# Fused attention and expert routing: score buffers in a fixed turn, and the fill between score groups by a written list

## The chip, the cores and the metric

The kernel runs on one core of a Trainium2 chip, in one launch. The metric is device time in microseconds. The kernel before was timed three times: 424.58, 422.84 and 422.7 us, median 422.84. The profile was taken in a further execution, whose own time was 424.22 us.

A core has five engines that run side by side, each through its own instructions in a fixed order: TensorE (PE: matmuls; PEld: its weight loads), VectorE (DVE), ScalarE (ACT), GpSimd (POOL) and SyncE (SP). They wait for one another by semaphores. Matmul results go to PSUM, which has eight banks.

## The reference

```python
# q, k, v: (8 batches, 8 heads, 1152, 64); w1: (8, 512, 1024); w2: (8, 1024, 512)
q_pool = q.reshape(B, H, S // 2, 2, D).mean(axis=3)          # 576 queries
scores = scale * q_pool @ k.transpose(0, 1, 3, 2)            # 576 x 1152
attn   = softmax(scores)                                     # (with exp(scores - max))
x      = (attn @ v), tokens x 512                            # 4608 tokens
for e in range(8):                                           # each token has one expert
    h = relu(x[domain_id == e] @ w1[e])
    out[domain_id == e] = h @ w2[e]
```

## The kernel before

**Attention.** Two heads form a pair; there are 32 pairs (4 to a batch), and each takes 12 steps of 432 score columns, 384 steps in all. One step is `score(t)` (PE: the keys' and queries' product for both heads, in the upper and lower half of the array, into a two-bank PSUM tile `s`) and `expo(t)` (ACT: one exponential over 2 x 432 columns from `s` into the SBUF tile `e`). The pool `spsum` holds three such two-bank tiles, so six of the eight banks. Once per pair `turn` transposes the next pair's keys and queries (30 transposes, L566) into one more `s` tile, and DVE copies them out (L571, L576).

**Products.** `av(p, h, c)` multiplies chunk c of the exponentials by the values (five matmuls, L619) into the single-bank tile `acc`; after nine chunks `evac` (DVE, L632 and L634) divides by the row sum, and `acc` is free for the next head.

**Expert work in the attention.** Tokens are sorted to 128-row tiles by expert, five per expert. Tiles whose tokens are in finished batches are gathered (POOL, `get_x`) and computed during the attention, in the remaining PSUM bank (tile `px`). One such tile is 17 pieces of PE work: one transposition (L783), eight `up` pieces (four matmuls each, L801) and eight `down` pieces (one matmul each, L814). After the transposition, after each four `up` pieces and after the last `down` piece DVE empties `px` (L786, L806, L820) before the next piece can start.

**What sets the order.** The program writes the PE's order as a loop over steps. Steps come in windows of two: both `score`s of a window stand together (L595; with the `turn` between them in the window that has it), then come three products and as many pieces as a planner allows. The planner (class `Fill` and the loop around `room`) keeps a sum of estimated costs per window and carries a debt. Products lag nine steps behind their scores (`AVS`), three in each window. `GET` holds the steps at which tiles are gathered. Scores use one tile form of PE (64 rows), products and pieces another (128 rows).

**After the attention** the remaining tiles run by expert in runs of one to five tiles: `stage1` (L1058, 32 matmuls a run for up to 512 columns), `stage2` (L1103, eight matmuls a tile), with tiles of coming runs transposed in between (L1076). 13 tiles are done in the attention, 27 after it, in runs of 3, 1, 2, 2, 2, 2, 3, 2, 5, 5.

Of the kernel before, what the change touches and what calls it, by code (L numbers as in the profile page):

```python
# [19 lines left out]
def kernel(  # L20
# [14 lines left out]
    E, _, F = moe_w1.shape  # L35
    NC = S // P
    NF = F // P
    ND = Dm // P
# [36 lines left out]
    spsum = att.enter_context(tc.tile_pool(name="spsum", bufs=3, space=bass.MemoryType.PSUM))  # L75
# [84 lines left out]
    pre = spsum.tile([P, 2, 512], FP32, name="s")  # L160
# [398 lines left out]
    def turn(p):  # L559
        kp, qp = kpt[p], qpt[p]  # L560
        new_kq(p)
        mt = spsum.tile([P, 2, 512], FP32, name="s")[:, :, :].bitcast(F16)
# [23 lines left out]
    def score(t):  # L586
        p, s_ = divmod(t, SPP)
        s = spsum.tile([P, 2, 512], FP32, name="s")
        st[t] = s
        o, u = 0, W * s_  # L590
        while o < W:
            c, q0 = divmod(u + o, Sp)
            n = min(Sp - q0, W - o)
            for r, (lo, hi) in enumerate(HALF):
                nc.tensor.matmul(  # L595
                    s[:, r, o : o + n], lhsT=kq[p][lo:hi, c * P : (c + 1) * P],
                    rhs=qz[p % 2][lo:hi, q0 : q0 + n], start=True, stop=True,
                )
            o += n
# [11 lines left out]
    def av(p, h, c, pool):  # L611
        if c == 0:
            if pool[0] is spsum:
                acc[p, h] = spsum.tile([P, 2, 512], FP32, name="s")[:, 0, :]
# [67 lines left out]
    def load_part(e, j):  # L682
# [6 lines left out]
    AVS = {9 + 2 * g: [(g // 3, c, ACC) for c in range(3 * (g % 3), 3 * (g % 3) + 3)] for g in range(6)}  # L689
    LAST = (spsum, "s")  # L690
    AVS_END = {
        8: [(0, c, ACC) for c in range(4)],
        10: [(0, c, ACC) for c in range(4, 6)],
        12: [(0, 6, ACC)] + [(1, c, LAST) for c in range(7)] + [(0, 7, ACC), (1, 7, LAST), (0, 8, ACC), (1, 8, LAST)],
    }
    STEP, C_MODE, C_S, C_T, C_AV, C_X, C_P, LAG = 771, 190, 183, 440, 147, 220, 217, 250
    SPAN = {2: 1420, 4: 1700, 6: 1260}
# [50 lines left out]
    class Fill:  # L748
        def __init__(self):
            self.blocks, self.cur, self.ready = [], None, 0  # L750

        def open(self):
            return self.cur is not None or (self.blocks and self.blocks[0][3])

        def piece(self):
            if self.cur is None:
                self.cur = list(self.blocks.pop(0))
            self.cur[0].pop(0)()
            if not self.cur[0]:
                self.ready = now[0] + self.cur[2]  # L760
                self.cur = None

        def able(self, t):
            b = self.blocks[0] if self.blocks else None
            return b and (b[3] or b[4].get("t", NST) < t < NST - 8 and t >= WSTEP[b[4]["xs"][0]][3] + 14)

        def turns(self, t):
            h0 = tiles[len(turned0)] if len(turned0) < len(tiles) else None
            if h0 and len(turned0) <= len(begun) and got.get(h0["xs"], NST) + 10 <= t < NST - 13:
                return h0  # L770
            return None

    fb = Fill()

    turned, turned0, begun, tiles = [], [], [], []
# [13 lines left out]
    def add_tile(e, i):  # L789
        h0 = {"xs": (e, i)}  # L790
        tiles.append(h0)
# [33 lines left out]

        for fn, lo, hi in ((up, 0, 4), (up, 4, NF), (down, 0, NF)):
            fb.blocks.append((
                [lambda f=f, fn=fn: fn(f) for f in range(lo, hi)], 222, 1, (fn, lo) != (up, 0), h0
            ))
# [5 lines left out]
    GET = [112, 118, 140, 168, 188, 208, 213, 230, 248, 266]  # L835
    want = [(e, i, at) for (e, i), at in zip(early, GET)]
    want += [(FILL, 0, 296), (0, 2, 304), (FILL, 1, 310), (FILL, 2, 316), (1, 2, 322), (2, 2, 328)]
    want += [(e, 2, 334) for e in range(3, E) if e != FILL]
# [46 lines left out]
    windows = {}  # L885
    for t in range(0, NST, 2):
        p, s_ = divmod(t, SPP)
        turns = [-(p + 1)] if s_ == (8 if p < 2 else 4) and p + 1 < NPAIR else []
        windows[t] = [t, *turns, t + 1]

    debt = 0
    for t in range(NST + 4):
# [14 lines left out]
        work_ns, span = 0, 0  # L907
        for it in windows.get(t, ()):
            if it < 0:
                turn(-it)  # L910
                work_ns += C_T
            else:
                score(it)
                expo(it)
                work_ns += C_S
                span += STEP
        if span:
            work_ns += C_MODE
            for off in (0, SPP):
                p0 = p - off // SPP  # L920
                if 0 <= p0 < NPAIR:
                    avs = AVS_END if p0 == NPAIR - 1 else AVS
                    work_ns += C_AV * sum(len(avs.get(s_ + off + d_, ())) for d_ in (0, 1))
            span = SPAN.get(s_, span) if 1 < p < NPAIR - 1 else span
        if t == 1:
            rest_k()
        for off in (0, SPP):
            p0 = p - off // SPP
            if 0 <= p0 < NPAIR:
                avs = AVS_END if p0 == NPAIR - 1 else AVS  # L930
                for h, c, bank in avs.get(s_ + off, ()):
                    av(p0, h, c, bank)
                    if c == NC - 1:
                        evac(p0, h)
                        if p0 % HP == HP - 1 and h == 1:
                            for i in range(NQ):
                                if p0 < NPAIR - 1:
                                    put[t + 1 + i] = (p0 // HP, i)
                                else:
                                    put_x(p0 // HP, i)  # L940

        if t == NST - 2 and not fb.open() and len(turned0) < len(tiles):
            x_ = tiles[len(turned0)]
            if got.get(x_["xs"], NST) + 10 <= t:
                x_["xt"] = fill.tile([P, ND, P], F16, name="xt0")
                turn_x(x_["xt"][:, :, :], *x_["xs"])
                turned0.append(x_["xs"])
                x_["t"] = t
        if t == NST + 1:
            while fb.open():  # L950
                fb.piece()
# [15 lines left out]
        while main and span:  # L967
            room = (180 if p > 1 and s_ in SPAN else LAG) + span - debt - work_ns
            if fb.cur is None:
                if t < fb.ready:  # L970
                    break
                x_, able = fb.turns(t), fb.able(t)
                if x_ and room >= C_X and not (able and room >= 2 * C_P):
                    x_["xt"] = fill.tile([P, ND, P], F16, name="xt0")
                    turn_x(x_["xt"][:, :, :], *x_["xs"])
                    turned0.append(x_["xs"])
                    x_["t"], fb.ready = t, t + 1
                    work_ns += C_X
                    break
                if not able:  # L980
                    break
            if room < C_P:
                break
            fb.piece()
            work_ns += C_P
# [377 lines left out]
```

## Time and profile before

| what | value |
|---|---|
| median of three runs | 422.84 us (422.7 to 424.58) |
| the profiled execution, own time | 424.22 us |
| its span, first to last instruction | 422.1 us |
| PE / ACT / DVE busy | 390.8 / 338.2 / 230.7 us |
| mean granted TensorE clock | 0.986 |
| last exponential ends | 315.99 us |
| first matmul of the last phase | 316.75 us |

The span divides in two at about 316 us: the attention, in which ACT is busy almost without a break, and the expert phase, in which PE is. Matmul times in the profile overlap and their ends are modelled; how long PE needs for a group is read from the start of one group to the start of the next. For ACT the time from the end of one exponential to the end of the next says more than the length of one, since consecutive ones overlap.

### The profile page before, as it was taken

How to read it: one execution, taken by the hardware profiler on the slowest of the kernel's cores; microseconds unless marked ns; L12 is line 12 of the kernel's file. 1: busy time of each engine (PE TensorE's matmuls, PEld its weight loads, DVE VectorE, ACT ScalarE, POOL GpSimd, SP SyncE). 2: the span in 40 equal slices, each digit the busy share in tenths (PEclk: the TensorE clock that was granted, in tenths of full speed). 3: DMA queues.
4: the chain of work that ended last, by engine and by line, in shares of the span. 5: the costliest groups of instructions: out<-in, count | busy, mean ns of one | idle time of the engine just before them, and what ended most of it. 6: DMA issues, size and time to landing. Idle time of an engine off the chain costs nothing.

```text
span 422.1 us, 14534 instructions
## 1 busy us (share of the span) xinstructions
PE 390.8 (93%) x6282; PEld 260.3 (62%) x6282; DVE 230.7 (55%) x635; ACT 338.2 (80%) x451; POOL 185.4 (44%) x303
## 2 busy tenths in 40 slices
PE   7888888888999999999999999999999999999992
PEld 4555555555766766766767667666675767555451
DVE  4588779884555565556565656556424345333231
ACT  5999999999999999999999999999992434323220
POOL 5542222423462734155423335644605888542422
PEclk9699999999999999999999999999999999999997
DMA  8999999994999999959689485986862697999302
GB/s 213 213 233 226 225 239 234 215 226 93 210 211 261 246 220 238 255 121 248 135 217 178 100 186 122 231 177 163 149 117 83 139 221 204 185 157 159 124 27 97
DMA packets 53134, 77.02 MB, mean 182 GB/s; under 512 B 12623, under 2 KB 41840, under 8 KB 53058
## 3 DMA queue, kind: packets, MB, share of 16 engines
q0 software_dynamic: 38336, 66.80, 78.1%
q1 hardware_dynamic: 14450, 9.06, 9.6%
q8 instruction: 51, 0.84, 0.8%
q14 instruction: 25, 0.20, 0.2%
q10 hardware_dynamic: 272, 0.13, 0.1%
HBM read 95.46 MB, written 15.21 MB: 262 GB/s over the span
## 4 chain that ended last, share of the span: by engine, by line
PE 44%; ACT 42%; issue 5%; DVE 4%; DMA 2%; POOL 1%; SPq 0%; POOLq 0%; ACTq 0%; DVEq 0%
ACT e L607 41%; PE hp L1058 11%; PE op L1103 11%; PE acc L619 7%; PE s L595 7%; PE px L801 3%; PE px L814 2%; DMA q<-in_q_dram 1%; DVE xb L634 1%; PE s L566 1%; PE hp L1076 1%; DMA x_tok<-xb 1%; DVE osb L452 0%; DVE h L440 0%; SPq L649 0%
## 5 line engine op out<-in xcount | busy, mean ns | idle before, releaser
L607 ACT ACTIVATE e<-s 128x864 f16<-128x864 f32 x384 | 305.1, 939 | 3.9 <-PE s L595 3.5
L595 PE MATMUL s<-qz,kq 64*128 64x432 f16 (+2 forms) x1152 | 119.9, 288 | 13.8 <-ACT e L607 10.3
L619 PE MATMUL acc<-v,e 128*128 128x65 f16 x2835 | 119.5, 194 | 4.9 <-DVE xb L634 4.1
L619 PEld LDWEIGHTS <-e 128*128 128x128 f16 x2880 | 104.2, 98 | 32.3 <-DVE xb L634 14.1
L595 PEld LDWEIGHTS <-kq 64*128 64x128 f16 x1152 | 48.6, 94 | 42.6 <-issue 24.7
L516 POOL DMA_INDIRECT out_dram<-osb,gid x40 | 42.2, 1056 | 72.8 <-DVE osb L820 38.9
L660 POOL DMA_INDIRECT xs<-x_tok,grow x40 | 42.8, 1069 | 69.8 <-DVE xs L94 26.8
L115 POOL DMA_DIRECT2D vs<-in_v_dram x32 | 23.8, 742 | 61.4 <-DVE v L541 28.9
L1103 PE MATMUL op<-w2h,hT 128*128 128x512 f16 x208 | 47.5, 379 | 0.0
L1058 PE MATMUL hp<-xt,w1h 128*128 128x256 f16 (+3 forms) x352 | 43.6, 282 | 0.2 <-ACT hT L1063 0.2
L1058 PEld LDWEIGHTS <-w1h 128*128 128x128 f16 x384 | 33.7, 98 | 15.8 <-DVE xs L94 0.4
L571 DVE COPY kq<-s 128x1152 f16<-128x1152 f16 x31 | 23.5, 757 | 34.5 <-PE s L566 34.5
L1065 DVE TENSOR_SCALAR hT<-hp 128x256 f16<-128x256 f32 (+3 forms) x40 | 20.7, 517 | 36.9 <-PE hp L1058 30.0
L1109 ACT COPY osb<-op 128x512 f32<-128x512 f32 x15 | 8.8, 586 | 39.6 <-PE op L1103 39.6
L1063 ACT ACTIVATE hT<-hp 128x256 f16<-128x256 f32 (+3 forms) x40 | 18.3, 459 | 24.3 <-PE hp L1058 24.2
L801 PE MATMUL px<-xt,w1h 128*128 128x128 f16 x416 | 34.0, 221 | 0.6 <-issue 0.6
L632 DVE RECIPROCAL cum<-acc 128x5 f32<-128x5 f32 x47 | 9.0, 191 | 43.9 <-PE acc L619 43.8
L1103 PEld LDWEIGHTS <-hT 128*128 128x128 f16 x208 | 19.8, 98 | 20.9
L814 PE MATMUL px<-w2h,h 128*128 128x512 f16 x104 | 32.3, 385 | 0.0
L801 PEld LDWEIGHTS <-w1h 128*128 128x128 f16 x416 | 23.4, 98 | 12.8 <-issue 12.8
L532 DVE TENSOR_TENSOR qp<-q 96x768 f16<-96x768 f32 x31 | 29.3, 946 | 2.4 <-DMA q<-in_q_dram 2.4
L806 DVE TENSOR_SCALAR h<-px 128x512 f16<-128x512 f32 x26 | 18.0, 691 | 15.2 <-PE px L801 14.2
(148 smaller groups left out, 337.3 us busy)
## 6 DMA issues: line engine op xcount, KB each, us to landing
q<-in_q_dram POOLq DMA_DIRECT2D x28, 576.0 KB
vs<-in_v_dram POOLq DMA_DIRECT2D x32, 288.0 KB
k<-in_k_dram POOLq DMA_DIRECT2D x31, 288.0 KB
w1h<-in_moe_w_dram POOLq DMA_DIRECT2D x16, 512.0 KB
w2h<-in_moe_w_dram POOLq DMA_DIRECT2D x16, 512.0 KB
x_tok<-xb SPq DMA_DIRECT2D x23, 96.0 KB, 6.0
q<-in_q_dram SPq DMA_DIRECT2D x3, 576.0 KB, 6.8
x_tok<-xb SPq DMA_DIRECT2D x23, 64.0 KB, 5.8
```

Of the source, the lines that this page charges most:

```text
L115: nc.gpsimd.dma_start(vs[:, :, :, :], v[b, h : h + 2].rearrange("h (p c) d -> p h c d", p=P))
L516: ins = nc.gpsimd.indirect_dma_start(out=dst[:, :], out_offset=bass.IndirectOffsetOnAxis(ap=ap, axis=0), in_=src, in_offset=None, **kw,)
L532: nc.vector.tensor_tensor(out=qp[0:QP, :, :, :].rearrange("p j h d -> p h j d"), in0=q2[:, :, :, 0:D], in1=q2[:, :, :, D : 2 * D], op=ALU.add,
L571: nc.vector.tensor_copy(kq[p][:, :].rearrange("p (c r k) -> p r c k", c=NC, r=2), mt[:, :, 0 : NC * 64].rearrange("p r (c k) -> p r c k", ...
L595: nc.tensor.matmul(s[:, r, o : o + n], lhsT=kq[p][lo:hi, c * P : (c + 1) * P], rhs=qz[p % 2][lo:hi, q0 : q0 + n], start=True, stop=True,)
L607: nc.scalar.activation(e_[:, :, o : o + W], st.pop(t)[:, :, 0:W], AF.Exp, bias=0.0, scale=0.0625)
L619: nc.tensor.matmul(acc[p, h][:, i * (D + 1) : (i + 1) * (D + 1)], lhsT=et[p, c // 3][:, h, o : o + P], rhs=v16[p % NV][:, c, h, 0 : D + 1] ...
L660: nc.gpsimd.indirect_dma_start(out=dst, out_offset=None, in_=x_dram[0 : 1 + nb * Sp, :], in_offset=bass.IndirectOffsetOnAxis(ap=ap, axis=0),)
L801: nc.tensor.matmul(m[:, f % 4, :], lhsT=wts[e][0][:, cc, f * P : (f + 1) * P], rhs=h0["xt"][:, cc, :], start=cc == 0, stop=cc == ND - 1,)
L814: nc.tensor.matmul(h0["o"][:, :], lhsT=h0["h"][:, f, :], rhs=wts[e][1][:, f, :], start=f == 0, stop=f == NF - 1,)
L1058: nc.tensor.matmul(hp_[:, lo : lo + n], lhsT=w1h[:, cc, f * P : (f + 1) * P], rhs=xt[:, cc, lo : lo + n], start=cc == 0, stop=cc == ND - 1,)
L1103: nc.tensor.matmul(op_[:, :], lhsT=hT[:, f, i * P : (i + 1) * P], rhs=w2h[:, f, :], start=f == 0, stop=f == NF - 1,)
```

## The change

The edit has three parts.

- **Buffers.** `spsum` has one buffer per name now, and three tiles s0, s1, s2 are made once; `next_s()` hands them out strictly in turn to scores, transposes and the last accumulators.
- **Order.** The planner, `AVS`, `AVS_END` and the cost constants are gone. From step 108 on a list of strings gives, for each window of two steps, what stands on PE: A is one product, P one piece (the transposition counts as one), a number repeats the letter before it, and what stands ahead of a slash goes between the window's two scores. Rows of six strings are one pair. Before step 108 each window has three products, as before. Two of its 23 lines are shown in the diff.
- **Tiles.** 14 tiles are computed in the attention, 26 after it, and some tiles are gathered at other steps (`GET`, `want`).

```diff
-    spsum = att.enter_context(tc.tile_pool(name="spsum", bufs=3, space=bass.MemoryType.PSUM))
+    spsum = att.enter_context(tc.tile_pool(name="spsum", bufs=1, space=bass.MemoryType.PSUM))
...
-    pre = spsum.tile([P, 2, 512], FP32, name="s")
+    sbuf = [spsum.tile([P, 2, 512], FP32, name=f"s{i}") for i in range(3)]
+    used = [1]
+    pre = sbuf[0]
+
+    def next_s():
+        used[0] += 1
+        return sbuf[(used[0] - 1) % 3]
...
-        mt = spsum.tile([P, 2, 512], FP32, name="s")[:, :, :].bitcast(F16)
+        mt = next_s()[:, :, :].bitcast(F16)
...
-        s = spsum.tile([P, 2, 512], FP32, name="s")
+        s = next_s()
...
+    PLAN0 = 108
+    PLAN = (
...
+        "A6 P3A3 A3 A2/PA P4A A4P "
+        "A4P2 P2A5 P2 A2/A2 P2A4 P5 "
...
+    ).split()
...
-    GET = [112, 118, 140, 168, 188, 208, 213, 230, 248, 266]
+    GET = [112, 124, 143, 162, 180, 208, 220, 238, 256, 274]
...
+        if main and t % 2 == 0:
+            line = PLAN[(t - PLAN0) // 2] if t >= PLAN0 else "A3" if t >= 8 else "-"
+            inner, _, line = line.rpartition("/")
+            score(t)
+            expo(t)
+            if s_ == (8 if p < 2 else 4) and p + 1 < NPAIR:
+                turn(p + 1)
+            steps(t, inner)
+            score(t + 1)
+            expo(t + 1)
+            steps(t, line)
...
+        if t == NST:
+            left = [u[1:] for u in units]
+            lead = [u for u in left if u < (0, 7)] + [u for u in left if (1, 0) <= u < (1, 7)]
+            for h, c in lead + [(0, 7), (1, 7), (0, 8), (1, 8)]:
+                product(t, (NPAIR - 1, h, c), LAST if h else ACC)
```

How the instructions stand at three places follows.

On PE, pair 23, steps 6 and 7 of the pair, so the first window behind the one with the transposes; `s` is the score tile, `kq` and `qz` the keys and queries, `px` a piece, `acc` a product, and the brackets name the engine whose semaphore is waited for. Before:

```order
L595 MATMUL s<-qz_100,kq 128x144
L595 LDWEIGHTS kq
L595 MATMUL s<-qz_100,kq 128x432 [waits Activation_49]
L595 LDWEIGHTS kq
L595 MATMUL s<-qz_100,kq 128x432
L814 LDWEIGHTS h_5479
L814 MATMUL px<-w2h,h_5479 128x512
L619 LDWEIGHTS e
L619 MATMUL acc<-v_0_103,e 128x65
```

Now (s_122 is the tile of step 6, s_123 the one into which the transposes went; ten product matmuls stand in the gap):

```order
L602 MATMUL s_122<-qz_100,kq 128x144
L626 LDWEIGHTS e
L626 MATMUL acc<-v_0_103,e 128x65
...
L602 LDWEIGHTS kq
L602 MATMUL s_123<-qz_100,kq 128x432 [waits DVE_49]
L602 LDWEIGHTS kq
L602 MATMUL s_123<-qz_100,kq 128x432
L626 LDWEIGHTS e
```

Step 7's score waited for an exponential (that of step 5) and directly followed step 6's; it now stands two products later, and waits for DVE's copies of the transposes instead.

On DVE, the same pair, around those copies (`kq`, `qz`); `cum` and `xb` are the division after nine products, `h` and `osb` empty `px`, `qp`, `v` and `kp` prepare coming pairs. Before:

```order
L541 COPY v_1_104<-vs 128x2x9x64
L547 COPY kp<-k_5232 128x2x9x64
L632 RECIPROCAL cum<-acc 128x5
L634 TENSOR_TENSOR xb<-acc,cum 128x5x64
L571 COPY kq<-s 128x2x9x64
L576 COPY qz_99<-s 128x6x64
L576 COPY qz_99<-s 128x6x32
L632 RECIPROCAL cum<-acc 128x5
```

Now:

```order
L548 COPY v_1_104<-vs 128x2x9x64
L554 COPY kp<-k_4967 128x2x9x64
L639 RECIPROCAL cum<-acc 128x5
L641 TENSOR_TENSOR xb<-acc,cum 128x5x64
L807 TENSOR_SCALAR h_5431<-px 128x512
L578 COPY kq<-s_123 128x2x9x64
L583 COPY qz_99<-s_123 128x6x64
L583 COPY qz_99<-s_123 128x6x32
L639 RECIPROCAL cum<-acc 128x5
```

In this pair one emptying of `px` has moved ahead of the copies; it belongs to pieces that stand five products and two scores ahead of the transposes on PE.

On ACT, in the last phase, the runs over experts 3 to 5 (`hT` after stage1 with the run's columns, `xt` a transposed tile, `osb` an output tile). Before:

```order
L1063 ACTIVATE hT<-hp 128x256 x4
L1082 COPY xt<-hp 128x4x128
L1109 COPY osb_8593<-op 128x512
L1063 ACTIVATE hT<-hp 128x384 x4
L1082 COPY xt<-hp 128x4x128
L1109 COPY osb_8671<-op 128x512
L1109 COPY osb_8707<-op 128x512
L1063 ACTIVATE hT<-hp 128x256 x4
L1109 COPY osb_8793<-op 128x512
```

Now:

```order
L1046 ACTIVATE hT<-hp 128x256 x4
L1065 COPY xt<-hp 128x4x128
L1092 COPY osb_8232<-op 128x512
L1046 ACTIVATE hT<-hp 128x256 x4
L1065 COPY xt<-hp 128x4x128
L1092 COPY osb_8331<-op 128x512
L1046 ACTIVATE hT<-hp 128x256 x4
L1092 COPY osb_8417<-op 128x512
```

The run over expert 4 has two tiles (256 columns) in place of three (384); the runs are 3, 1, 2, 2, 2, 2, 2, 2, 5, 5 now.

## Rows read from the trace of the kernel before

**Rows 1.** The page: busy us, share of the span and instructions of each engine.
```profile
PE 390.8 (93%) x6282; PEld 260.3 (62%) x6282; DVE 230.7 (55%) x635; ACT 338.2 (80%) x451; POOL 185.4 (44%) x303
```

**Rows 2.** Busy us (count) by engine, two stretches; then PEclk, DMA share, GB/s.
```profile
27.00:103.00 76.00, 64.40 (x1306) 42.30 (x1303) 60.63 (x208) 75.95 (x98) 23.14 (x33) 1.00 1.05 212
103.00:316.00 213.00, 206.94 (x4001) 145.46 (x3998) 119.69 (x286) 210.36 (x265) 94.65 (x142) 1.00 0.90 189
```

**Rows 3.** Timeline of ACT: start us, us taken, work xcount, idle before it and releaser.
```profile
36.03 29.89 ACT L607 ACTIVATE e<-s 128x864 f16<-128x864 f32 x38
...
102.14 5.71 ACT L607 ACTIVATE e<-s 128x864 f16<-128x864 f32 x7
...
161.35 4.88 ACT L607 ACTIVATE e<-s 128x864 f16<-128x864 f32 x6 [0.38 <-PE s L595]
166.87 28.62 ACT L607 ACTIVATE e<-s 128x864 f16<-128x864 f32 x36 [0.63 <-PE s L595]
...
292.01 23.98 ACT L607 ACTIVATE e<-s 128x864 f16<-128x864 f32 x30 [0.18 <-PE s L595]
```

**Rows 4.** Timeline of PE, DVE and ACT in one pair, from 239.66 us.
```profile
239.66 0.54 PE L595 MATMUL s<-qz,kq 64*128 64x288 f16 x6
...
240.13 0.40 PE L801 MATMUL px<-xt,w1h 128*128 128x128 f16 x4
...
241.29 0.43 PE L566 MATMUL s<-ident,kp 64*128 64x64 f16 x18
...
241.93 0.76 DVE L571 COPY kq<-s 128x1152 f16<-128x1152 f16 x1 [0.68 <-PE s L566]
242.05 0.36 PE L595 MATMUL s<-qz,kq 64*128 64x144 f16 x4 [0.16 <-ACT e L607]
...
242.34 0.62 PE L801 MATMUL px<-xt,w1h 128*128 128x128 f16 x8
242.61 0.51 DVE L576 COPY qz<-s 128x384 f16<-128x384 f16 x2
...
242.80 0.61 PE L619 MATMUL acc<-v,e 128*128 128x65 f16 x15
...
243.35 0.63 PE L595 MATMUL s<-qz,kq 64*128 64x288 f16 x6
243.75 2.46 ACT L607 ACTIVATE e<-s 128x864 f16<-128x864 f32 x3 [0.18 <-PE s L595]
```

**Rows 5.** Timeline of PE, two places where it stopped for "issue".
```profile
160.28 0.23 PE L801 MATMUL px<-xt,w1h 128*128 128x128 f16 x1 [0.57 <-issue]
...
166.48 0.54 PE L595 MATMUL s<-qz,kq 64*128 64x288 f16 x5 [0.18 <-issue]
```

**Rows 6.** Timeline of PE in the last phase, a run of three tiles and one of two.
```profile
361.91 5.36 PE L1058 MATMUL hp<-xt,w1h 128*128 128x384 f16 x32
367.11 0.39 PE L1076 MATMUL hp<-ident,xs 128*128 128x128 f16 x4
367.33 1.89 PE L1103 MATMUL op<-w2h,hT 128*128 128x512 f16 x8
...
372.74 3.66 PE L1058 MATMUL hp<-xt,w1h 128*128 128x256 f16 x32
376.23 3.62 PE L1103 MATMUL op<-w2h,hT 128*128 128x512 f16 x16
```

**Rows 7.** Timeline of PE where the attention ends.
```profile
313.92 0.54 PE L595 MATMUL s<-qz,kq 64*128 64x288 f16 x6
...
316.59 0.31 PE L619 MATMUL s<-v,e 128*128 128x65 f16 x5
316.75 1.46 PE L1058 MATMUL hp<-xf,w1h 128*128 128x384 f16 x8
```

**Rows 8.** Timeline of POOL at a weight load; DMA queue share, 150 to 180 us.
```profile
160.49 0.83 POOL L506 DMA_DIRECT2D w2h<-in_moe_w_dram  x1
...
q0 software_dynamic: 3978, 6.49, 104.9%
```

More of the change, by code (lines that the diff above doesn't have):

```diff
@@ L613, in av @@
             if pool[0] is spsum:
-                acc[p, h] = spsum.tile([P, 2, 512], FP32, name="s")[:, 0, :]
+                acc[p, h] = next_s()[:, 0, :]
             else:
@@ L746 @@
     now = [0]
[L748 to L775, printed above, removed]
+    turned, begun, blocks, cur = [], [], [], []
     def spare(shape, dt=FP32):
@@ L790, in add_tile, with flip @@
         h0 = {"xs": (e, i)}
-        tiles.append(h0)
+        def flip():
+            h0["xt"] = fill.tile([P, ND, P], F16, name="xt0")
+            turn_x(h0["xt"][:, :, :], e, i)
         def up(f):
@@ L824, in down, with piece, product, steps @@
                 done[e] = i + 1
+        blocks.append([flip])
         for fn, lo, hi in ((up, 0, 4), (up, 4, NF), (down, 0, NF)):
-            fb.blocks.append((
-                [lambda f=f, fn=fn: fn(f) for f in range(lo, hi)], 222, 1, (fn, lo) != (up, 0), h0
-            ))
+            blocks.append([lambda f=f, fn=fn: fn(f) for f in range(lo, hi)])
+    def piece():
+        if not cur:
+            cur.extend(blocks.pop(0))
+        cur.pop(0)()
+    units = [(p, h, c) for p in range(NPAIR) for h in range(2) for c in range(NC)]
+    def product(t, u, pool):
+        p, h, c = u
+        av(p, h, c, pool)
+        if c == NC - 1:
+            evac(p, h)
+            if p % HP == HP - 1 and h == 1:
+                for i in range(NQ):
+                    if p < NPAIR - 1:
+                        put[t + 1 + i] = (p // HP, i)
+                    else:
+                        put_x(p // HP, i)
+    def steps(t, line):
+        kind = None
+        for ch in line + ".":
+            if ch.isdigit():
+                n = int(ch)
+            if kind and not ch.isdigit() or ch == ".":
+                for _ in range(n if kind else 0):
+                    piece() if kind == "P" else product(t, units.pop(0), ACC)
+                kind = None
+            if ch in "AP":
+                kind, n = ch, 1
     early = [(0, 0), (1, 0), (2, 0), (3, 0), (4, 0), (0, 1), (1, 1), (2, 1), (3, 1), (4, 1)]
@@ L883, in plan_runs @@
         runs.extend((e, 0, NTC) for e in range(FILL + 1, E))
[L885 to L891, printed above, removed]
     for t in range(NST + 4):
@@ L906 @@
             (load_k if s_ == 2 else load_v)(p + 3)
[L907 to L924, printed above, removed]
+        if main and t % 2 == 0:
[9 more added lines that the diff above has]
+            steps(t, line)
@@ L925 @@
         if t == 1:
             rest_k()
[L927 to L948, printed above, removed]
+        if t == NST:
[3 more added lines that the diff above has]
+                product(t, (NPAIR - 1, h, c), LAST if h else ACC)
@@ L949 @@
         if t == NST + 1:
-            while fb.open():
-                fb.piece()
+            while cur or blocks and len(begun) and len(blocks) % 4:
+                piece()
             plan_runs()
@@ L966 @@
             flip_x(xt[0][:, :, i * P : (i + 1) * P], e, i)
[L967 to L985, printed above, removed]
-        debt = max(0, debt + work_ns - span) if span else debt + work_ns
         if t == 8:
```

34 lines of the change are left out of this document (24 added, 10 removed).

## The prediction

> **What bounds the kernel now.** I read the page first. PE is busy for 390.8 of 422.1 us and ACT for 338.2 [rows 1], but as means over two phases. So I looked at the stretches next: from 103 to 316 us ACT is busy for 210.4 of 213.0 us and PE for 206.9, at a granted clock of 1.00; from 27 to 103 us, with no expert work in the attention, PE is busy for 64.4 of 76.0 us and ACT for all of it [rows 2]. Up to 316 us, then, exponentials set the pace; behind it PE does, whose groups follow one another without a break [rows 6].
>
> The third view is ACT alone. 38 exponentials in an unbroken row take 29.89 us [rows 3]; the first takes about 0.92, so 28.97 / 37 = 0.783 us from end to end. That is ACT's floor. From 102.14 to 292.01 + 23.98 = 315.99 us it does 265 of them [rows 2, 3]: 213.85 us, where the floor gives 264 x 0.783 + 0.92 = 207.6. ACT loses 6.2 us here, and the fourth view says to whom: the idle time in front of its rows ends with PE's scores [rows 3, 4].
>
> One loss recurs, in the window behind the transposes. Step 5's score starts at 242.05, held back by ACT: the transposes took one of three buffers, so it needs that of an exponential just ended. From there PE needs 0.29 to the next work, 0.46 for two pieces and 0.55 for three products with the switch of tile form, and step 6's score stands at 243.35 [rows 4]. ACT starts on it 0.40 later, after 0.18 of idle time; three exponentials after a break take 2.46 = 0.89 + 2 x 0.783, so a break costs its idle time and another 0.11, here 0.29 [rows 4]. Work of 0.91 us stood between the two scores, so 0.62 would have fitted. Two larger losses, 0.38 and 0.63 of idle time at 161.35 and 166.87, follow PE's own stops for "issue" [rows 3, 5]. I book 1.0 us to these and 5.2 to the order of the work.
>
> **The change, part by part.** Prices on PE, from the start of one group to that of the next [rows 4]: two scores and the switch out 0.47 (239.66 to 240.13), the switch in 0.10 (0.55 for 15 product matmuls, which at 0.03 each make 0.45), so 0.57 for a window's scores; a product 0.15; a piece 0.23 (0.46 for two).
>
> *Order behind the transposes.* The list puts three products (0.45), two pieces (0.46) or a piece and a product (0.38) there, where up to 0.91 stood. All are under 0.62: the recurring break goes. Next late could be step 7's score. Before, it waited for exponential 5; by the rows of the order it waits for DVE's copies now. In pair 24's times step 6's score would stand at 242.05 + 0.29 + 0.45 + 0.10 = 242.89 and step 7's, after two products, at 242.89 + 0.29 + 0.30 + 0.10 = 243.58. The copies end at 242.61 + 0.51 = 243.12 [rows 4]: 0.46 to spare.
>
> *Other windows.* The second score of a window can start when the exponential three steps back ends; the next window's first score must be ready three exponentials later, 2.35. Off this go 0.05 for the start, 0.29, 0.10, 0.40 to ACT's start and 0.11: 1.40 of work fits. The list's fullest entry there, two pieces and five products, is 0.46 + 0.75 = 1.21.
>
> *PE's load.* Pairs 10 to 31 before: 132 windows x 0.57 = 75.2; 21 groups of transposes at about 0.5 = 10.5 (from 241.29 on, rows 4); 396 products x 0.15 = 59.4; 13 tiles x 17 pieces x 0.23 = 50.8; together 196 of 213.85. Added: 17 pieces, 3.9, and 21 slashes in these pairs, each with a second switch out and in, 0.20, so 4.2. That makes 204 against ACT's 207.6. ACT's exponentials hide all of it, with 3.6 us left over; without that cover it would cost its 8.1 us.
>
> The Trainium skill (TensorEngine Tiling (Array Packing), Key Properties) says that changing the tiling mode drains TensorE, which speaks against 21 more changes. The trace agrees that a change costs something, 0.10 each way; a whole drain, put at the 0.2 or so by which a product's matmul outlasts its start-to-start time, would come to 0.4 a slash, 8.4 in all, and leave PE with nothing to spare.
>
> *Buffers.* The strict turn adds no instruction on PE. It moves a wait (above), and step 8 and 9 then wait for exponentials 5 and 6, which they are early enough for.
>
> *A tile less at the end.* The run of three tiles over expert 4 becomes one of two. stage1 of three starts at 361.91 and ends at 367.11, 5.20; of two, 372.74 to 376.23, 3.49. A transposed tile takes 0.22 (367.11 to 367.33), and a tile of stage2 half of 3.62 less the overlap, 1.73. So 1.71 + 1.73 + 0.22 = 3.7 us go [rows 6]. PE has no break there, so nothing else takes its place; between 0 (a gather or load becomes the wait) and 3.7 I take 3.7.
>
> *The seam.* After the last score 14 products and one piece take PE to 316.75, 0.76 after ACT's end [rows 7]. Now five pieces stand there, 0.9 more; the score itself may come up to 0.4 earlier. I take 0.5 later (0 to 0.9).
>
> *What stays.* Products that need the newest exponential, emptied banks, a stop for "issue": of 5.2 I leave 0.6 (bounds 0 and 5.2).
>
> Sum: -5.2 + 0.6 - 3.7 + 0.5 = -7.8. The profiled execution took 424.22 us, 2.1 beside its span, and is 1.4 above the median; its two stops for "issue" are about that. So I take the sum off the median: 422.84 - 7.8 = **415.0 us**. From the profiled one it is 424.22 - 1.0 - 7.8 = 415.4.
>
> **Rivals.**
>
> 1. *The wait only moves.* With products and pieces in bunches, PE may wait for `acc` or `px` to be emptied, or for a product's exponential. For it: DVE is in order, and one bank each serves products and pieces. Against: the list always puts other work behind a ninth product or a fourth piece. Half of the gain or none: 418 to 422.84 - 3.7 + 0.5 = 419.6; I say 418.
>
> The Trainium skill (ScalarE: Activation LUTs, What ACT_TABLE_LOAD costs) would make it the whole: an activation with immediates takes 186 ns and 0.833 ns per element, less about 93 of overlap, an estimated 813 ns for 864 columns. 264 of them are 215 us, more than was measured, and no stall would be left to recover: 419.6. The trace disagrees, with 0.783; I give this 2 in 100, inside the rival.
>
> 2. *Expert 4's weights are late.* Its pieces start eight to ten steps sooner, while the load's steps stand. The last part is issued at 160.49, in a stretch whose DMA queue is at 104.9% [rows 8]; its first use moves from step 218 to step 212, from about 181 to 174 us (166.87 is step 198 [rows 3], PE is two steps ahead, and some 2 us are saved by then). For a late landing: the queue; against: 13 us are left. If it lands only where it was used before, PE and then ACT stop for up to 7 us; with 6 it is 421.
>
> 3. *The other side: the copies become the wait.* If DVE ends the copies over 0.46 later than now, step 7's score is late, and from 0.73 ACT stalls (0.26 is its own lead there: 2.35 after exponential 3's end at about 242.0, less 0.5, is 243.85). An emptying of `px` (0.7) and a division (0.7) in front would make it 1.4, so 0.67 in 21 pairs: +14. Without the 5.2: 422.84 - 3.7 + 0.5 + 14 - 5.2 = 428, and no longer faster from 0.40 us a pair. For: in pair 23 an emptying has moved ahead of the copies. Against: it hangs on pieces five products and two scores earlier on PE, and DVE was idle for 0.68 before its copies [rows 4].
>
> 4. *The change doesn't do what it says.* Waits on the same exponentials under new names: then step 7 would wait for ACT as before, and the gain of the order is about halved: 417.5. The order's rows speak against it.
>
> **How the numbers follow.** The forecast 62 in 100, its own range 413.4 to 416.5; rival 1 with 20, rival 2 with 8, rival 3 with 5, rival 4 with 5. The range for 8 in 10 is 413.2 (nothing stays, the seam costs nothing: 422.84 - 8.9 = 413.9, and 0.7 for runs and early windows) to 419.2, short of the end of rival 1. About half a per cent, 2.1 us, is what a measurement here can tell from no change. Faster (below 420.7): the forecast, rivals 1 and 4 and a part of rival 2, 0.89; same 0.06; slower 0.05.
>
> **What would show it.** Right: ACT's unbroken rows grow past 36 exponentials, ending near 311 us; no idle time in front of step 6; 14 x 8 `down` matmuls in the attention; the last phase 3.7 us shorter. Wrong: ACT idle before step 7 with DVE as what ended it (rival 3), PE idle at `px` or `acc` (rival 1), a single break of microseconds near 164 to 175 us (rival 2). If PE is packed without a break and ACT still waits, the prices of switches or pieces were too low.

## The result

The changed kernel took 417.40 us (median of four runs, 417.0 to 417.66), the kernel before 422.86 (four runs, 422.7 to 424.58): estimated ratio 0.9845, 95% interval 0.9811 to 0.9879 (the two medians divide to 0.987). Measured again later, it was 418.28 against 423.07, ratio 0.9879 (0.9858 to 0.9900). The forecast was 415.0 with an own range of 413.4 to 416.5: the gain came, 2.4 us smaller than its sum, and both times lie above that range, inside the wider one of 413.2 to 419.2. By the number alone they are closer to rival 4 (417.5) and rival 1 (418); only the traces below tell them apart.

In the experiments, two executions that took longer than the others of their kernel at a lower granted clock (450.95 us at 0.969, 588.22 at 0.558) are left out of the times given.

The page of the kernel after, busy us by engine, answers to [rows 1]; the two stretches below it (busy us, then PEclk, DMA share, GB/s) to [rows 2].

```profile
PE 388.5 (94%) x6314; PEld 259.2 (62%) x6314; DVE 232.3 (56%) x638; ACT 334.6 (81%) x450; POOL 181.8 (44%) x303
```

```profile
27.00:103.00 76.00, 66.01 (x1311) 43.48 (x1309) 61.68 (x209) 76.00 (x98) 22.28 (x32) 1.00 1.06 212
103.00:316.00 213.00, 209.97 (x4088) 146.38 (x4086) 123.95 (x301) 208.87 (x266) 94.06 (x148) 1.00 0.91 191
```

PE is now the busier engine of the second stretch. ACT's busy time there holds the start of the last phase too, so its share says little. Its timeline does (start us, us taken, count, idle before and releaser), against [rows 3]:

```profile
99.39 19.77 ACT L614 ACTIVATE e<-s 128x864 f16<-128x864 f32 x25
119.39 192.41 ACT L614 ACTIVATE e<-s 128x864 f16<-128x864 f32 x244 [0.22 <-PE s L602]
```

The breaks of every ten to thirty exponentials are gone; 244 exponentials stand in one row. It ends at 311.80, where it was 315.99. The 269 exponentials take 212.41 us; the floor of 0.783 gives 268 x 0.783 + 0.92 = 210.76. So 1.65 us are still lost, in breaks too short for a row of their own, and at the one stop of PE for "issue" that this execution had:

```profile
118.45 0.39 PE L815 MATMUL px<-w2h,h 128*128 128x512 f16 x1 [0.46 <-issue]
```

What PE waited for from 100 to 313 us (us in total, times, longest) is little, and no wait for `acc` or `px` to be emptied is among it:

```profile
PE s L602 <- ACT e L614: 1.8, 8, 0.4
PE px L815 <- issue: 0.5, 1, 0.5
PE s L602 <- DVE qz L583: 0.3, 1, 0.3
```

Pair 24 on PE, DVE and ACT answers to [rows 4]:

```profile
238.97 0.43 PE L573 MATMUL s<-ident,kp 64*128 64x64 f16 x18
...
239.47 0.36 PE L602 MATMUL s<-qz,kq 64*128 64x144 f16 x4
239.68 0.76 DVE L578 COPY kq<-s 128x1152 f16<-128x1152 f16 x1 [0.71 <-PE s L573]
...
239.77 0.40 PE L781 MATMUL px<-ident,xs 128*128 128x128 f16 x4
...
240.00 0.31 PE L626 MATMUL acc<-v,e 128*128 128x65 f16 x5
...
240.26 0.36 PE L602 MATMUL s<-qz,kq 64*128 64x288 f16 x4
240.35 0.51 DVE L583 COPY qz<-s 128x384 f16<-128x384 f16 x2
240.55 0.32 PE L626 MATMUL acc<-v,e 128*128 128x65 f16 x5
...
240.92 0.36 PE L602 MATMUL s<-qz,kq 64*128 64x432 f16 x2
```

Step 5's score stands at 239.47, step 6's at 240.26: 0.79 later, where it was 1.30. One transposed tile and one product lie between. Step 7's score stands at 240.92, right after the copies' end at 240.86, and ACT did not stop here.

The end of the attention answers to [rows 7]:

```profile
309.40 0.54 PE L602 MATMUL s<-qz,kq 64*128 64x288 f16 x6
309.88 1.25 PE L815 MATMUL px<-w2h,h 128*128 128x512 f16 x5
...
312.94 0.31 PE L626 MATMUL s<-v,e 128*128 128x65 f16 x5
313.10 0.81 PE L1041 MATMUL hp<-xf,w1h 128*128 128x384 f16 x4
314.54 4.72 PE L1041 MATMUL hp<-xf,w1h 128*128 128x384 f16 x28 [0.62 <-DVE xs L94]
```

The first `stage1` starts 1.30 us after ACT's end (0.76 before) and then stops after its first four matmuls: it takes 6.00 us (313.10 to 319.10) instead of 5.35. The row names a memory set on DVE; the wait in the program is on the division of the last pair's second sums just ahead of it, which ended at 314.48.

The last phase answers to [rows 6]. The run of three tiles is a run of two. But expert 6's `stage1` has a stop that was not there:

```profile
358.68 3.66 PE L1041 MATMUL hp<-xt,w1h 128*128 128x256 f16 x32
362.18 0.39 PE L1059 MATMUL hp<-ident,xs 128*128 128x128 f16 x4
...
373.02 1.03 PE L1041 MATMUL hp<-xt,w1h 128*128 128x512 f16 x4
374.29 7.99 PE L1041 MATMUL hp<-xt,w1h 128*128 128x128 f16 x60 [0.24 <-DMA xt<-xs]
382.12 2.11 PE L1086 MATMUL op<-w2h,hT 128*128 128x512 f16 x9
```

Between the two profiled executions (424.22 and 417.45, spans 422.1 and 415.3) the 6.8 us come from, to 0.1:

| where | us |
|---|---|
| ACT's last exponential (315.99 to 311.80) | -4.2 |
| seam (0.76 to 1.30) | +0.5 |
| first `stage1` (5.35 to 6.00) | +0.7 |
| the tile (run of three to run of two) | -3.7 |
| expert 6's `stage1` (8.69 to 9.09) | +0.4 |
| behind the last matmul (7.56 to 7.01) | -0.6 |

The execution of before carried two stops for "issue" [rows 5] worth about 1.2 us; without them it is 5.6, close to the medians' 5.5. The shorter end behind the last matmul is luck: over the versions profiled on chips of this speed it is 7.0 to 7.8 us.

### The profile page after: what moved, and what is told of

It reads as the page before. It is cut to its first block, busy times and chain, and to the rows that moved or that the text cites. A ratio compares the mean times of both kernels' runs of the same rounds, so it can differ in the third digit from the quotient of the medians.

```text
span 415.3 us, 14651 instructions
## 1 busy us (share of the span) xinstructions
PE 388.5 (94%) x6314; PEld 259.2 (62%) x6314; DVE 232.3 (56%) x638; ACT 334.6 (81%) x450; POOL 181.8 (44%) x303
## 4 chain that ended last, share of the span: by engine, by line
PE 42%; ACT 37%; DMA 8%; DVE 5%; issue 5%; POOL 1%; POOLq 0%; SPq 0%; ACTq 0%; DVEq 0%
ACT e L614 36%; PE s L602 8%; PE acc L626 8%; PE hp L1041 8%; PE op L1086 8%; DMA k<-in_k_dram 4%; DMA xt<-xs 3%; PE px L802 3%; PE px L815 3%; PE s L573 1%; DVE kq L578 1%; DMA out_dram<-osb,gid 1%; POOL out_dram L523 1%; DVE qz L583 1%; PE hp L1059 1%
## 5 line engine op out<-in xcount | busy, mean ns | idle before, releaser
L602 PE MATMUL s<-qz,kq 64*128 64x432 f16 (+2 forms) x1152 | 121.5, 289 | 10.9 <-ACT e L614 8.4
L626 PEld LDWEIGHTS <-e 128*128 128x128 f16 x2880 | 101.8, 98 | 37.6 <-issue 21.9
L626 PE MATMUL acc<-v,e 128*128 128x65 f16 x2835 | 120.9, 194 | 3.1 <-DVE xb L641 2.9
L667 POOL DMA_INDIRECT xs<-x_tok,grow x40 | 39.8, 995 | 104.1 <-DVE xs L94 37.4
L602 PEld LDWEIGHTS <-kq 64*128 64x128 f16 x1152 | 47.0, 94 | 42.8 <-issue 24.0
L1086 PE MATMUL op<-w2h,hT 128*128 128x512 f16 x200 | 45.8, 379 | 0.0
L1041 PEld LDWEIGHTS <-w1h 128*128 128x128 f16 x384 | 33.7, 98 | 15.2 <-DVE xs L94 1.0
L1041 PE MATMUL hp<-xt,w1h 128*128 128x256 f16 (+2 forms) x352 | 42.0, 277 | 0.4 <-DMA xt<-xs 0.2
L802 PE MATMUL px<-xt,w1h 128*128 128x128 f16 x448 | 32.5, 220 | 0.0
L802 PEld LDWEIGHTS <-w1h 128*128 128x128 f16 x448 | 25.4, 98 | 4.8 <-issue 4.8
```

Of the source, the lines that this page charges most:

```text
L602: nc.tensor.matmul(s[:, r, o : o + n], lhsT=kq[p][lo:hi, c * P : (c + 1) * P], rhs=qz[p % 2][lo:hi, q0 : q0 + n], start=True, stop=True,)
L626: nc.tensor.matmul(acc[p, h][:, i * (D + 1) : (i + 1) * (D + 1)], lhsT=et[p, c // 3][:, h, o : o + P], rhs=v16[p % NV][:, c, h, 0 : D + 1] ...
L667: nc.gpsimd.indirect_dma_start(out=dst, out_offset=None, in_=x_dram[0 : 1 + nb * Sp, :], in_offset=bass.IndirectOffsetOnAxis(ap=ap, axis=0),)
L802: nc.tensor.matmul(m[:, f % 4, :], lhsT=wts[e][0][:, cc, f * P : (f + 1) * P], rhs=h0["xt"][:, cc, :], start=cc == 0, stop=cc == ND - 1,)
L1041: nc.tensor.matmul(hp_[:, lo : lo + n], lhsT=w1h[:, cc, f * P : (f + 1) * P], rhs=xt[:, cc, lo : lo + n], start=cc == 0, stop=cc == ND - 1,)
L1086: nc.tensor.matmul(op_[:, :], lhsT=hT[:, f, i * P : (i + 1) * P], rhs=w2h[:, f, :], start=f == 0, stop=f == NF - 1,)
```

## The experiments

The experiments fell on four chips. On two of them the kernel before takes 423 us, on two 441. What was measured on one kind is compared only within it. The changed kernel itself ran only where the kernel before takes 423.

**The buffers alone.** The kernel before, with its three pool buffers replaced:

```diff
-        s = spsum.tile([P, 2, 512], FP32, name="s")
+        s = next_s()
```

> The kernel before, with its planner and thirteen tiles, but with the three score buffers taken strictly in turn. Theory (the order of the work carries the gain in the attention): 0.91 us of work still stands between the scores of steps 5 and 6, so the breaks stay, the last exponential ends near 316 us, and the strict turn by itself gives nothing. It costs 0.6 at the end of the attention, where the last pair's second sums now lie in the bank that the second group of the next phase takes: 423.4 us (422.6 to 424.2). Rival (the buffers carry a part, as step 7's score no longer waits for an exponential): up to half of the 4.6, 421 us or less.

442.15 us where the kernel before took 440.79: ratio 1.0014 (0.9985 to 1.0042). ACT's timeline has the old pattern of breaks:

```profile
195.95 11.13 ACT L613 ACTIVATE e<-s 128x864 f16<-128x864 f32 x14 [0.19 <-PE s L601]
207.51 7.94 ACT L613 ACTIVATE e<-s 128x864 f16<-128x864 f32 x10 [0.43 <-PE s L601]
215.62 11.16 ACT L613 ACTIVATE e<-s 128x864 f16<-128x864 f32 x14 [0.17 <-PE s L601]
```

14 and 10 exponentials make the 24 of two pairs. The strict turn by itself gives nothing there; the first `stage1` took 6.00 us, as the theory had it.

**The list without the strict turn,** the same edit undone in the changed kernel, twice:

> The changed kernel with its list and fourteen tiles, but with the pool of before handing out the score buffers. Theory: step 7's score waits for exponential 5 again, which ends 0.1 us or so after PE would be ready, while ACT wants that score only 0.3 us later than that; PE waits, ACT doesn't: 417.4 us (416.8 to 418.2), last exponential near 311.8. Rival 4 of the prediction put the price of this wait at half of the order's gain, 2.3 us: 419.7.

> The changed list and tile with the pool of before, once more, beside the kernel before. Where the kernel before takes about 423: theory (step 7's wait for exponential 5 costs PE a little and ACT nothing) 418.3 us, within 0.7 of the changed kernel; rival 4's price 420.5. Where it takes about 440, as in the first call: ratio 1.007 again.

Both runs fell where the kernel before takes 441: 442.99, ratio 1.0070 (1.0046 to 1.0093), and 441.28, 1.0022 (1.0000 to 1.0043). The wait on ACT is there, as read from the order (first run, 100 to 323 us: us in total, times, longest):

```profile
PE s L596 <- ACT e L608: 5.5, 13, 0.8
```

It cannot be priced, since the changed kernel itself was not run on such a chip; its nearest relative, the last experiment's version, had 12.7 us of lost time on ACT in pairs 10 to 31 there against 11.7 and 14.0 here. By these profiles no half of the gain hangs on the turn. The times do not say so clearly: beside the second run that version took 443.78, 2.5 us more, though the two profiled spans are alike (441.0 and 441.1). So the order's share is shown in the traces, and what the strict turn adds or costs stays open.

**Both scores adjacent** (one of the 23 rows):

```diff
-        "A6 P3A3 A3 A2/PA P4A A4P "
+        "A6 P3A3 A3 A2PA P4A A4P "
```

> The changed kernel with the 23 slashes of the list taken out: both scores of every window are adjacent, and the work that stood between them follows the second. Theory (PE has time to spare, and the copies are in time): step 7's score waits for DVE's copies for 0.1 us or so in its pairs, ACT is not held up, and the 4.2 us of switches that PE saves are worth nothing to the end: 417.4 us (416.8 to 418.2). Rival A (the split hides a real wait for the copies): a break of 0.2 to 0.3 us in 21 pairs, 4 to 6 us more, 422. Rival B (a switch costs a whole drain and PE is at its limit): 1 us or more is given back, 416.4 or less.

447.50, ratio 1.0147 (1.0108 to 1.0187): 4.5 us above the list with the pool on the same chip. My theory fell, and on that chip rival A holds in kind: the split covers a real wait for the copies.

```profile
PE s L602 <- DVE qz L583: 9.1, 16, 1.4
```

```profile
PE s L603 <- DVE qz L584: 4.4, 6, 1.1
```

The second line is a version with the split on the other chip of 441 (the first run of the last experiment). The breaks are not the 0.2 to 0.3 us in 21 pairs that rival A named: step 8 was 0.5 late in pairs 13, 16 and 24 (0.35 with the split), and the rest is spread over many steps. Where the kernel before takes 423 this was not tried.

**The work between steps 6 and 7 moved ahead of step 6** (one of the 18 rows):

```diff
-        "A6 P3A3 A3 A2/PA P4A A4P "
+        "A6 P3A3 A3A2 PA P4A A4P "
```

> The changed kernel with the work that the list puts between the scores of steps 6 and 7 moved ahead of step 6's score in 18 pairs. There the window behind the transposes then holds 0.75 us of work in 13 pairs and 0.53 in 5, where 0.62 should fit. Theory: 13 breaks of 0.13 + 0.11 us in front of step 6, 3.1 us: 420.5 (419.8 to 421.5), the idle time ended by PE's scores. Rival (the limit of 0.62 is wrong, and what counts is the window as a whole): no more than 0.5 us, 417.9 or less.

443.42, ratio 1.0076 (1.0040 to 1.0111), only 0.4 us above the list with the pool on the same chip: the time does not show it. The trace does. Breaks appear in front of step 6: in pairs 11, 14, 17, 19, 22 and 25, with five products in the window, the end of step 6's exponential came about 0.15 us late, with two pieces and two products 0.05 to 0.14; in the run with the pool it was 0 in each of these. The place is right; the price had been put at 0.24. With 0.11 for the break itself, an estimated 0.71 us of work fits (0.75 - 0.04), not 0.62.

**The changed kernel again,** as control:

> The changed kernel unaltered, as the control beside the kernel before and the three edits of this call; the first four edits ran on a chip on which the kernel before took 440.8 us instead of 422.8. Theory 1 (the gain is in the order and the tile, whatever the chip): 5.5 us below the kernel before in the same call, ratio 0.985 to 0.99. Theory 2 (where transfers are slower, DVE's copies for step 7 come late and take the gain back, as rival 3 had it): where the kernel before takes about 440, the ratio is 0.995 or more and PE waits for the copies in many pairs.

418.28, ratio 0.9879: theory 1 holds there, and theory 2 could not be tried on such a chip. Its first `stage1` took 6.00 again, and expert 6's `stage1` 10.68:

```profile
372.26 1.03 PE L1041 MATMUL hp<-xt,w1h 128*128 128x512 f16 x4
375.11 7.99 PE L1041 MATMUL hp<-xt,w1h 128*128 128x128 f16 x60 [1.83 <-DMA xt<-xs]
```

The four tiles of its first 512 rows were there; the fifth transposing load landed only at 375. What held these loads back stands in SP's waits of the changed kernel from 340 us on (us in total, times, longest):

```profile
SPq L1281 <- DVE hT L1048: 35.7, 1, 35.7
```

L1281 is SP's load of the check word, which needs all divisions of the attention summed up; it started at 352.6 and was done at 353.3, and the ten loads stood behind it in SP's queue: the first starts at 353.55.

**The banks rotated.**

```diff
+    sbuf = sbuf[2:] + sbuf[:2]
     pre = sbuf[0]
```

> The changed kernel with the three score buffers renamed in rotation, so that the last pair's second sums lie in the bank that the third group of the next phase takes, as before the change, and not the second. Theory (the 0.66 us of the first stage1 is PE's wait for DVE's division of these sums): the first stage1 takes 5.35 us instead of 6.00, and the time is 0.6 us below the control. Rival (it is the late second half of expert 5's weights): no difference, stage1 at 6.0.

The first `stage1` is one unbroken row of 5.35 us, 315.28 to 320.63:

```profile
315.28 5.51 PE L1042 MATMUL hp<-xf,w1h 128*128 128x384 f16 x32
```

The mechanism is shown. The time, 418.19 (ratio 0.9873, 0.9849 to 0.9896), does not show it beside the control's 418.28: the profiled execution, 421.03, stopped on PE for 1.71 us at 119 and waited 1.85 us for expert 6's loads.

```profile
119.10 0.39 PE L816 MATMUL px<-w2h,h 128*128 128x512 f16 x1 [1.71 <-issue]
```

**Pair 2's keys copied three steps later.**

```diff
-        if t in (12, 16):
-            (prep_k if t == 12 else prep_q)(2)
+        if t in (15, 16):
+            (prep_k if t == 15 else prep_q)(2)
```

> The changed kernel with the copy of pair 2's keys moved from step 12 to step 15 in DVE's order, behind the first routing work. Theory (in pair 1 DVE stood for 4.6 us in front of this copy until the keys landed at 20.5 us, so the routing work, the division and the copies for step 11's score came late): the break of 0.8 us in front of pair 1's last exponential is gone, 0.5 to 0.9 us below the control. Rival (the break is the order of PE or the strict turn alone): the break stays, within 0.2 us of the control.

419.13 (ratio 0.9908, 0.9876 to 0.9939); inconclusive, because what it was to mend was chance. In the first execution of the changed kernel these keys landed at 20.5 us and ACT stopped for 0.77 in pair 1; in the control they landed at 17.2, and pair 1 lost nothing without the edit.

**Thirteen tiles.** The last 17 `P` of the list left out:

> The changed kernel with the last 17 pieces left out of its list, so that the fourteenth tile (expert 3's third) is done in the last phase, in a run of two tiles over one expert. Theory (a tile in the attention is free, at the end it costs 3.7 us): 3.7 us above the control less at most 0.5 for the seam, where five pieces fewer stand behind the last score: 3.2 to 3.7. Rival (PE was at its limit with fourteen tiles): the attention gets shorter by as much, 1 us or less above the control.

420.22 (ratio 0.9937, 0.9914 to 0.9960) against the control's 418.28: 1.9 us, 1.1 between the profiled spans, not 3.2 to 3.7. In the profile the run of three is back, 5.20 us for its `stage1` and 3.45 for the two tiles of `stage2` that follow it, and expert 6 waits for nothing:

```profile
357.04 5.36 PE L1041 MATMUL hp<-xt,w1h 128*128 128x384 f16 x32
...
364.42 3.62 PE L1086 MATMUL op<-w2h,hT 128*128 128x512 f16 x16
...
374.82 8.86 PE L1041 MATMUL hp<-xt,w1h 128*128 128x512 f16 x64
```

Where the control gained 3.73 by the tile it gave back 1.99 at expert 6's loads, 0.55 at the seam (1.31 against 0.75) and 0.40 at the bank; the rest of the 1.1 is 0.5 behind the last matmul. The last exponential ended at 310.88, in the control at 311.02: the fourteenth tile cost the attention 0.1 us.

**Up pieces doubled.**

```diff
-            for cc in range(ND):
+            for cc in [*range(ND)] * (2 if f in (1, 5) else 1):
```

> The changed kernel with two of the eight up pieces of each tile done twice over, 28 pieces of 0.22 us, 6.2 us of PE's time in pairs 10 to 31 that nothing needs. Theory of the prediction's load sum (3.6 us of PE's time are left over): 2.6 us more, 420.9 where the changed kernel takes 418.3, with ACT's idle time ended by PE's scores. Rival A (PE is at its limit, a switch costs more than 0.10): the whole 6.2, 424.5. Rival B (more room than the sum says): 1 us or less.

446.94 (ratio 1.0145, 1.0122 to 1.0169), on a chip where the kernel before took 440.57. In pairs 10 to 31 ACT lost 17.6 us, 12.7 in the last experiment's version on the same chip: 4.9 of the 6.2 us reached ACT. So an estimated 1.3 us were left over, not 3.6. That is rough, since one and the same kernel (the list with the pool) lost 11.7 and 14.0 in its profiles on the two chips of 441, and it holds where PE's results also came late (last section); on the other chips this was not tried.

**Both waits of the last phase removed.** The rotation, and:

```diff
-    tx = ... tile_pool(name="tx", bufs=3 ...)
+    tx = ... tile_pool(name="tx", bufs=2 ...)
+    ts = ... tile_pool(name="ts", bufs=2 ...)
...
-        for kn in (k_ + 1, k_ + 2):
+        for kn in (k_ + 1, k_ + 2, k_ + 3):
...
-            xt[kn] = new_xt()
+            xt[kn] = new_xt() if kn >= FLIP else ts.tile([P, ND, 2 * P], F16, name="xts")
```

with the gathers (`fetch`) one run earlier as well. That puts the ten loads ahead of the check word in SP's order.

> The changed kernel with two edits in what follows the attention: the rotation of the score buffers (second group of the first stage1 free at once), and the ten transposing loads of experts 6 and 7 issued earlier, each expert into a buffer of its own and ahead of SP's load of the check word, so that they wait for their gathers alone. Theory (the 3.7 us of the tile came in short by two waits, 0.66 at the second sums' bank and 0.4 to 2.0 at expert 6's fifth transposing load): first stage1 5.35 us, expert 6's stage1 8.69 us, and 1.0 to 2.6 us below the changed kernel: about 416.5 where the kernel before takes 423, ratio 0.985. Rival (the earlier transposing loads only push the weights' and gathers' transfers back): a wait of the same size at expert 5's or 6's weights, within 0.7 us of the changed kernel.

> The version with the two edits behind the attention once more, since its first run fell on the chip on which the kernel before takes 440 us and on which PE stopped for 4 to 6 us in the last phase of every kernel, so that expert 6's transposing loads were not what it waited for. Where the kernel before takes 423: theory, first stage1 5.35 us, expert 6's stage1 8.69 us, 1.0 to 2.6 us below the 418.3 of the changed kernel, ratio to the kernel before 0.981 to 0.986; rival (the loads only push others back), 417.6 or more with a new wait at a weight load. Where the kernel before takes 440: ratio 1.009 as in the call before.

The first run fell on a chip of 441: 443.78, ratio 1.0088 (1.0054 to 1.0122). There PE stopped in the last phase of every version, for 1.8 to 6.3 us at the longest, so that expert 6 waited for nothing anyway. The second: 416.28 (416.01 to 420.19) against 423.00, ratio 0.9854 (0.9822 to 0.9885). In its profile, 414.3 us of span, SP's row of the ten loads starts at 316.54, in the changed kernel at 353.55 (SP's queue: start, us taken). Three of the five loads of expert 6 start by 319.1, the other two, which wait for their gathers, at 348.7 and 351.4; in the changed kernel these two start at 358.5 and 359.8.

```profile
316.54 45.88 SPq L683 DMA_TRANSPOSE xt<-xs  x10
```

```profile
353.55 26.89 SPq L682 DMA_TRANSPOSE xt<-xs  x10
```

and PE goes through expert 6 in one row of 8.69 us, 371.58 to 380.27:

```profile
371.58 8.86 PE L1043 MATMUL hp<-xt,w1h 128*128 128x512 f16 x64
```

From the first `stage1` to the last matmul it takes 94.26 us; the changed kernel took 95.23 and 96.82, the kernel before 97.84. Of the tile's 3.7 us, 3.6 are there. It has the lowest median, 1.1 and 2.0 us below the two of the changed kernel, and the stalls are gone in the trace; but its ratio lies between the two of the changed kernel (0.9845 and 0.9879), so the times alone don't prove it.

## Why the prediction was right and where it fell short

*What bounds the kernel.* Right: exponentials up to the end of the attention, then PE. Nothing moved that.

*The order behind the transposes.* Right in mechanism: the break in front of step 6 went, by the order and not by the buffers, and putting work back there brought it back (the last two as traces on the chips of 441 show it). Mis-sized: the forecast had -5.2 + 0.6 = -4.6, the traces have 6.13 us lost in pairs 10 to 31 before, about 1.23 of it at the two stops, and 1.58 and 1.39 in the two profiles after: -3.3 to -3.5. The term that fell short is *What stays*, 0.6.

About 1.1 us comes again at the same steps in all six profiles of versions with the list and the strict turn on chips of 423. In pair 13 step 8's exponential is 0.23 to 0.26 late, behind step 7's score, which waited 0.3 for DVE's copies: rival 3's mechanism. In pairs 14, 17, 22, 25 and 30 step 0's is 0.05 late and step 4's 0.04. Smaller ones stand in pairs 21 and 29; in pair 21 step 7 waited 0.12 for the copies too.

In front of these late steps 0 stand windows of two products and four pieces, 1.22 us by the prediction's prices (which it had missed in naming 1.21 as the fullest), so "1.40 of work fits" failed. It is no matter of a lower limit, though. The same entry at the end of pairs 10, 18 and 26 cost nothing in the changed kernel, nor did the 1.21 of two pieces and five products in pairs 15, 20, 23 and 28. Where the 1.22 cost 0.05, the next score started 0.52 ahead of the last exponential's end; where it cost nothing, 0.64. So the lead that PE brings from the windows before counts too, and the prediction took each window by itself. For the window behind the transposes its limit erred the other way, 0.62 instead of an estimated 0.71.

The rest of what stayed is chance, another 0 to 0.9 us in five of the profiles and once 3.3: PE's stops for "issue", and the copies again, for which PE waited 0.3 in pair 24 in three of the six profiles and in pair 16 in one, with ACT 0.3 late each time.

*Step 7 against the copies.* "0.46 to spare" was too much: in pair 24 there was 0.06. One product stands between the scores, where I had counted two (0.15), and step 5's score, no longer held back by ACT, starts 0.50 behind the transposes, where I had kept the 0.76 of before. It held in this execution; in three of the other profiles pair 24 came 0.3 late, so this margin was luck. Taking the split away showed the same nearness on a chip of 441.

*PE's load.* ACT hid the tile's 3.9 us, as its cost of 0.1 in the attention shows; of the 4.2 us for the slashes no run on a chip of 423 tells more than that ACT lost 1.6 in all. The 3.6 us left over were not confirmed: a rough 1.3 where it was measured, on a chip of 441.

*The strict turn* "adds no instruction on PE" and moves a wait, as forecast. It also moved the last pair's second sums from the bank of the third group of the next phase to that of the second. The edit hands out these last accumulators too, and I did not follow them past the attention: +0.66.

*The tile* is worth 3.7 us, shown from both sides. What failed is "PE has no break there, so nothing else takes its place". The bound "a gather or load becomes the wait" stood in the text at 0; the truth lay between. The five transposing loads of expert 6 start when the check word in front of them in SP's queue is done, which comes ahead of the run that got shorter: they started 3.0 us earlier than before (353.55 against 356.56), but were wanted 6.7 us earlier (373.02 against 379.68). Before, the fifth landed at 376.6, 3.1 us ahead of its use; now it landed at 374.3, when PE already stood waiting for it. This took back 0.4, 0.46, 1.83 and 1.99 us in four executions.

The Trainium skill (VectorE: DVE Perf Modes, The three transpose paths) puts a 128x128 bf16 transpose at 1309 ns by DMA and 390 ns by TensorE, an estimated 5.2 us for the four in such a load. The changed kernel's trace has 2.7 us apiece in SP's row and 3 to 9 between landings, 4.4 on average (356.75 to 374.25 for five), against 0.22 of PE's time for a tile. By either, five loads need far longer than the 3.7 us by which the phase shrank, so the page's comparison should have made me look for their start.

*The seam* cost 0.55 (0.5 forecast). *The rivals*: ACT lost 0.1 us from 164 to 175 us, so the weights of expert 4 were in time; the wait did not move to `px` or `acc`; step 7's score waits for the copies and not for ACT, as the order says.

In sum, against -7.8: +1.3 (order), +0.4 (a later first exponential, and late keys in pair 1), +1.1 (bank and loads), -0.6 (a shorter end behind the last matmul) make -5.6. The +0.4 and the -0.6 are chance. Without the waits at the bank and the loads it was 416.3.

## What to carry to other kernels

When a stage in front of a load gets shorter, follow the load back to what starts it: that PE "has no break there" now is no price for the next wait, and the load's start may hang on something unrelated ahead of it in its queue. When buffers are renamed or dealt in another order, follow each bank into the next phase, to whoever takes it over. A limit for work that "fits" is worth testing by putting work back: one such limit was off by 0.1 us here. And it is no limit for one window alone, since a late start is carried over from the window before.

## What the runs showed of the hardware

The gain depends on the chip. On two chips the kernel before takes 441 us, and no version with the list was faster than it (ratios 1.002 to 1.015); the changed kernel itself was not among them. The kernel before with the strict turn, profiled there, lost 11.2 us on ACT in pairs 10 to 31, the versions with the list 11.7 to 17.6. Two things differ in these traces from those of the other chips; the granted clock is 1.00 from 27 us to the end of the attention on both.

PE's results reach the others late, at nearly the same steps in each version with this list. In pair 13, on such a chip (the version with both waits removed):

```profile
134.25 0.34 PE L574 MATMUL s<-ident,qp 64*128 64x64 f16 x12
134.43 0.35 PE L603 MATMUL s<-qz,kq 64*128 64x144 f16 x4
...
135.64 2.53 ACT L615 ACTIVATE e<-s 128x864 f16<-128x864 f32 x3 [0.49 <-PE s L603]
135.65 0.76 DVE L579 COPY kq<-s 128x1152 f16<-128x1152 f16 x1 [1.81 <-PE s L603]
...
136.89 0.36 PE L603 MATMUL s<-qz,kq 64*128 64x432 f16 x2 [1.07 <-DVE qz L584]
```

On the control's chip PE's rows there are the same to 0.04 us, and DVE's copy starts at 134.82. PE's records, whose ends are modelled, show no gap up to here; DVE sees the result 0.8 us later, and ACT, idle for 0.49, starts at the same moment. In this version ACT loses 1.0 to 1.7 us in each of pairs 13, 16, 20, 23, 24, 26 and 29. That a list without spare room has to pay for each of these is my reading, not shown by a run.

And in the last phase PE stops, here with no wait named:

```profile
366.82 3.59 PE L1043 MATMUL hp<-xts,w1h 128*128 128x256 f16 x16 [6.30 <-issue]
```

The granted clock was 1.00 before and well into it, 0.70 from 364 to 366 us and 0.50 (1.2 GHz) from 366 to 370: the stop came first. The others saw results late here too: DVE copied a tile at 366.33 whose transposes are recorded from 358.40; in the same version on a chip of 423 the same copy stands 0.8 us behind them (341.09 and 340.28). So both differences may be one, with PE held up earlier than its records say; no run separates them.

The Trainium skill (Runtime: NRT & Kernel Launch, Instruction fetch mechanics) says that an engine's sequencer fetches its instructions in 16 KiB blocks by a DMA queue of its own, "mostly hidden". This trace has a queue of that kind, 51 packets of 16 KB of 0.9 to 2.0 us each; stops at fixed places of a program would fit it. But most of the packets' times don't stand at the stops, and no run here took such a fetch away: the cause is open.
